# Attention with beacons and a gated MLP on one core: merged softmax sums, shared product banks, early score chunks in the ring, and a new order

## The chip, the cores and the metric

One core of a Trainium2 chip runs the whole program. The metric is the device time of one execution in microseconds; the time of the kernel before is the median of three runs.

## The reference

Eight batches of eight heads attend over 576 tokens of 64 channels, with 16 beacon keys and values in front that every query sees; the heads are laid side by side, and an MLP with a sigmoid-gated activation follows.

```python
B, H, S, Nb, D = (8, 8, 576, 16, 64)
k_all = np.concatenate([beacon_k, k], axis=2)
v_all = np.concatenate([beacon_v, v], axis=2)
scores = scale * np.matmul(q, k_all.transpose(0, 1, 3, 2))   # causal beyond the beacons
a = np.exp(scores); a /= a.sum(-1, keepdims=True) + 1e-09
attn = np.matmul(a, v_all)                                   # -> x: 4608 x 512
h = x @ w_in                                                 # 512 x 2048
g = h * (1.0 / (1.0 + np.exp(-1.702 * h)))
out = g @ w_out                                              # 2048 x 512
```

## The kernel before

**Work and tiles.** The kernel computes in f16 with sums in f32. Attention goes in 16 sets of four heads (two sets a batch). Per set, the loads bring keys, queries (`kn`, `qn`) and values (`vb`), cast on the way by POOL's DMA queue; DVE transposes them to `kT`, `qT`, and casts and transposes the beacon keys (`e_bk`, `e_turn`). The scores are computed transposed (keys on partitions, queries on columns), in chunks of 512 columns for four heads at once (L484): 32 rows of the array per head, four heads side by side. A chunk lies in one tile `s` of four PSUM banks; ACT takes the exp of it into `E` (L495), and the next chunk waits for that. Masks are cut in by POOL (L516), for the first sets partly by DVE (L509). The value products and the softmax sums (L571, operands `vb` or `ones`) use 32 columns of the array per head. DVE turns the sums out of PSUM (L583), takes reciprocals (L590), spreads them (L594), and normalises the products into `xT` (L606).

From the fifth set on (`s >= EARLY`) the key blocks of `E` are first added on DVE (`e_zadd`, L534), and a set's sums are two products, one for queries 0 to 223 and one for 224 to 575, each with its own transpose, reciprocal and spread.

**The MLP** runs in groups of tokens, two of 256 and then of 512. `w_in` products (L630) go through a gate: for the first two groups tanh on ACT (L644) and a product on DVE (L663), later a Gelu activation (L651), which needs another table in ACT than exp. The second product is plain for the first two groups (L675). For the others it is a 2x2 scheme with seven products in place of eight (`products`, L744): DVE builds sums of the quarters (`e_s`, L695), each of products 1 to 7 fills a PSUM bank of its own, and DVE adds the banks into output tiles (`e_half` on ACT, `e_join` at L760), from where SP stores them. The last three groups use such a scheme for `w_in` too (`fast`: L831, L841, L850, L853, L859).

**PSUM** has eight banks: a ring of four (`u0` to `u3`) for sums, value and MLP products, and four for `s`, which join the ring once the last chunk is done.

**Order.** Every operation is entered in a plan with its engine, a duration and its dependencies. `ORDER` lists each engine's operations in the order in which they are emitted; the list was made beforehand, and `Plan.run` only merges the five lists by planned times and gives out the banks. So the order on each engine is fixed in the code, and an engine that waits holds up all behind it. POOL's queue holds the loads too: each waits for the one eight places before it to land.

**Fill.** Matmuls on a constant tile (L1326) are put ahead of the first two chunks: 72 of 112 columns and 2 of 256 columns in f32.

Of the kernel before, what the change touches and what calls it, by code (L numbers as in the profile page):

```python
# [7 lines left out]
F16 = mybir.dt.float16  # L8
F32 = mybir.dt.float32
# [8 lines left out]
        76, 100, 115, 118, 120, 106, 138, 141, 143, 108, 155, 111, 152, 129, 161, 158, 122, 131, 164, 167, 134, 127,  # L18
        170, 173, 176, 145, 125, 148, 150, 177, 182, 188, 191, 227, 194, 197, 232, 183, 203, 234, 200, 178, 237, 179,
        206, 258, 241, 209, 184, 263, 185, 212, 265, 213, 248, 246, 268, 214, 215, 401, 251, 253, 272, 218, 404, 275,  # L20
        244, 279, 219, 220, 407, 282, 284, 277, 221, 414, 320, 296, 304, 290, 302, 292, 300, 298, 312, 308, 294, 318,
        314, 310, 306, 316, 426, 435, 423, 343, 338, 339, 340, 433, 431, 438, 344, 345, 359, 349, 341, 464, 346, 350,
        351, 352, 354, 574, 355, 429, 360, 361, 577, 356, 362, 357, 372, 365, 583, 474, 477, 373, 366, 374, 367, 605,
        480, 484, 375, 482, 607, 368, 506, 502, 488, 492, 610, 490, 486, 498, 504, 500, 508, 514, 510, 516, 494, 496,
        512, 534, 593, 596, 535, 536, 539, 540, 550, 541, 542, 537, 742, 545, 546, 547, 548, 603, 745, 551, 552, 553,
        599, 601, 619, 622, 748, 555, 556, 557, 558, 561, 755, 625, 627, 629, 562, 563, 776, 568, 564, 569, 570, 571,
        779, 764, 767, 659, 637, 641, 657, 649, 651, 647, 661, 635, 631, 653, 805, 772, 770, 774, 643, 655, 633, 639,
        645, 679, 680, 815, 818, 700, 681, 682, 684, 701, 915, 690, 685, 686, 691, 692, 702, 918, 687, 693, 695, 703,
        696, 924, 821, 823, 697, 698, 706, 946, 825, 707, 713, 708, 709, 948, 934, 937, 714, 715, 716, 827, 951, 944,
        940, 942, 853, 831, 833, 855, 857, 851, 843, 835, 837, 847, 839, 845, 829, 849, 841, 1083, 960, 963, 875,  # L30
        876, 880, 877, 878, 881, 882, 1086, 968, 966, 970, 883, 1089, 902, 909, 903, 886, 891, 1096, 887, 888, 889,
        892, 893, 1117, 904, 894, 905, 896, 897, 1120, 898, 899, 910, 911, 1105, 1108, 1146, 912, 976, 994, 996, 972,
        978, 1000, 1002, 992, 984, 990, 986, 988, 974, 980, 982, 998, 1168, 1111, 1115, 1159, 1113, 1156, 1025, 1026,
        1020, 1027, 1171, 1021, 1022, 1028, 1023, 1031, 1177, 1032, 1033, 1164, 1166, 1162, 1199, 1034, 1036, 1047,
        1048, 1037, 1201, 1041, 1042, 1038, 1039, 1233, 1049, 1204, 1043, 1044, 1050, 1235, 1237, 1054, 1055, 1056,
        1057, 1239, 1249, 1190, 1241, 1265, 1251, 1242, 1253, 1255, 1187, 1245, 1267, 1258, 1281, 1257, 1269, 1216,
        1195, 1197, 1193, 1213, 1261, 1271, 1285, 1287, 1283, 1273, 1289, 1274, 1219, 1221, 1223, 1334, 1290, 1293,
        1277, 1357, 1335, 1313, 1318, 1314, 1336, 1315, 1319, 1316, 1320, 1321, 1373, 1324, 1325, 1337, 1326, 1329,
        1327, 1361, 1377, 1375, 1330, 1359, 1340, 1331, 1341, 1332, 1363, 1342, 1366, 1365, 1379, 1381, 1347, 1382,
        1348, 1369, 1389, 1385, 1349, 1343, 1395, 1393, 1391, 1405, 1350, 1397, 1398, 1409, 1437, 1407, 1411, 1413,  # L40
        1401, 1414, 1481, 1438, 1417, 1497, 1442, 1443, 1444, 1483, 1439, 1440, 1499, 1487, 1501, 1485, 1458, 1445,
        1459, 1460, 1489, 1513, 1490, 1448, 1453, 1449, 1450, 1451, 1454, 1503, 1455, 1493, 1505, 1461, 1456, 1464,
        1465, 1517, 1515, 1506, 1529, 1519, 1509, 1466, 1471, 1522, 1472, 1473, 1521, 1533, 1467, 1474, 1582, 1525,
        1535, 1537, 1531, 1538, 1561, 1566, 1562, 1541, 1588, 1567, 1589, 1563, 1564, 1568, 1569, 1572, 1590, 1573,
        1574, 1575, 1591, 1577, 1578, 1595, 1579, 1580, 1583, 1584, 1585, 1596, 1597, 1598,
    ],
    "ACT": [
        1, 3, 77, 79, 103, 101, 107, 109, 112, 153, 156, 130, 159, 162, 132, 165, 168, 135, 171, 174, 189, 192, 228,
        195, 198, 233, 235, 201, 204, 238, 180, 207, 259, 210, 264, 186, 266, 269, 216, 402, 405, 408, 222, 417, 415,
        297, 291, 303, 305, 301, 299, 293, 309, 321, 295, 319, 313, 315, 311, 307, 317, 436, 439, 342, 465, 468, 575,  # L50
        578, 584, 587, 606, 608, 503, 507, 489, 491, 493, 487, 499, 505, 509, 515, 517, 495, 501, 511, 497, 513, 611,
        538, 743, 746, 749, 756, 758, 777, 780, 660, 642, 638, 652, 658, 648, 650, 636, 632, 662, 654, 806, 644, 634,
        656, 640, 646, 809, 916, 683, 919, 928, 925, 947, 949, 952, 828, 832, 854, 856, 852, 858, 834, 838, 844, 840,
        836, 846, 830, 848, 850, 842, 1084, 879, 1087, 1090, 1099, 1097, 1118, 1121, 1147, 1150, 977, 995, 997, 973,
        979, 1001, 993, 985, 991, 989, 1003, 975, 981, 987, 983, 999, 1169, 1172, 1024, 1181, 1178, 1200, 1202, 1234,
        1205, 1236, 1238, 1240, 1250, 1252, 1244, 1266, 1254, 1256, 1268, 1248, 1246, 1264, 1270, 1260, 1282, 1262,
        1272, 1286, 1284, 1288, 1276, 1280, 1292, 1294, 1296, 1278, 1358, 1317, 1374, 1378, 1376, 1360, 1362, 1364,
        1372, 1380, 1368, 1370, 1384, 1390, 1386, 1396, 1394, 1406, 1388, 1392, 1410, 1408, 1412, 1404, 1400, 1416,
        1402, 1482, 1418, 1420, 1498, 1484, 1500, 1441, 1486, 1488, 1496, 1492, 1502, 1504, 1494, 1514, 1516, 1508,
        1518, 1520, 1512, 1510, 1530, 1528, 1534, 1524, 1526, 1536, 1532, 1540, 1544, 1542, 1565,  # L60
    ],
    "DVE": [
        73, 74, 75, 97, 98, 99, 80, 81, 82, 78, 116, 105, 87, 104, 117, 102, 121, 119, 139, 140, 144, 142, 157, 154,
        123, 163, 160, 124, 224, 169, 128, 166, 172, 175, 146, 147, 126, 149, 151, 225, 226, 398, 190, 193, 196, 199,
        255, 256, 257, 202, 205, 286, 242, 411, 287, 211, 208, 243, 399, 249, 247, 400, 250, 412, 254, 252, 273, 245,
        274, 280, 276, 413, 281, 285, 283, 278, 289, 461, 288, 462, 419, 580, 420, 463, 326, 327, 328, 421, 322, 92,
        323, 324, 422, 427, 428, 424, 425, 325, 330, 334, 329, 335, 432, 336, 331, 434, 337, 332, 333, 470, 347, 582,
        353, 471, 581, 472, 430, 473, 358, 363, 475, 476, 478, 479, 481, 485, 739, 483, 369, 376, 370, 589, 752, 740,
        590, 615, 518, 753, 921, 519, 754, 526, 591, 527, 520, 528, 592, 529, 521, 741, 522, 597, 523, 594, 530, 595,
        598, 531, 802, 532, 524, 533, 616, 543, 525, 604, 549, 617, 618, 554, 600, 620, 602, 623, 624, 621, 559, 760,  # L70
        628, 761, 762, 626, 630, 565, 763, 566, 768, 572, 765, 811, 812, 766, 803, 804, 769, 773, 771, 671, 1080,
        775, 672, 813, 922, 663, 814, 664, 675, 667, 816, 673, 819, 668, 669, 817, 923, 665, 666, 820, 674, 676, 677,
        1093, 670, 688, 694, 678, 930, 822, 824, 699, 931, 826, 932, 933, 704, 710, 938, 939, 935, 936, 717, 711,
        945, 941, 943, 1081, 956, 957, 958, 871, 1082, 1094, 1095, 959, 872, 873, 1225, 867, 859, 961, 962, 964, 965,
        860, 863, 1174, 1143, 861, 874, 862, 868, 864, 967, 865, 971, 866, 969, 884, 869, 870, 1101, 1144, 890, 1145,
        1102, 895, 1226, 1103, 1104, 900, 906, 1109, 907, 1110, 913, 1106, 1107, 1152, 1153, 1227, 1176, 1175, 1154,
        1012, 1004, 1005, 1155, 1006, 1112, 1116, 1008, 1160, 1016, 1013, 1009, 1157, 1161, 1007, 1114, 1158, 1017,
        1010, 1011, 1014, 1029, 1018, 1183, 1165, 1163, 1019, 1229, 1015, 1230, 1035, 1228, 1231, 1167, 1184, 1040,
        1232, 1209, 1045, 1185, 1051, 1052, 1186, 1058, 1210, 1191, 1243, 1192, 1247, 1211, 1212, 1188, 1189, 1263,
# [28 lines left out]
    ],  # L108
}


class Op:
    __slots__ = (
        "eng", "dur", "deps", "pr", "due", "emit", "kind", "ring", "mode", "lat",
# [4 lines left out]
class Plan:  # L119
# [30 lines left out]
    def run(self):  # L150
# [25 lines left out]
        while any(todo.values()):  # L176
            first = None
            for e, seq in todo.items():
# [15 lines left out]
                if first is None or t < first[0]:  # L194
                    first = t, e, i
# [1162 lines left out]
```

## Time and profile before

| | |
|---|---|
| median of 3 runs | 324.87 us (324.68 to 325.06) |
| profiled execution | 324.84 us, of which the span of its instructions 323.1 us |
| mean granted TensorE clock | 0.992 |
| busy: PE, DVE, ACT, POOL | 312.2 (97%), 261.7 (81%), 219.5 (68%), 113.4 (35%) us |
| table loads of ACT | 14, of 1283 ns |
| first score chunk, first MLP matmul | 8.27 us, 17.21 us |

PE is TensorE's matmul, PEld its weight loads, DVE VectorE, ACT ScalarE, POOL GpSimd, SP SyncE. A line of the profile names the source line, the engine, the operation, output and inputs, the shape and the count, then busy time or start and duration, and in brackets the idle time before it and what ended that.

### The profile page before, as it was taken

The numbers are of one execution on the slowest core, as the hardware profiler recorded it, in microseconds if no ns is written. First come the engines' busy times: TensorE is split into PE (matmuls) and PEld (weight loads), VectorE is DVE, ScalarE is ACT, GpSimd is POOL, SyncE is SP. The second block draws the span as 40 slices with busy tenths as digits, with TensorE's granted clock in tenths as the row PEclk, the third lists the DMA queues.
The fourth block names the chain that finished last, engine by engine and source line by source line (L and its number), as shares of the span: only waits on it lengthen the run. The fifth ranks groups of instructions, "written<-read, shape, count | busy, mean of one in ns | idle before, by whom it ended". The sixth has DMA issues, their size and how long they took to land. (4 is left out here: it accounts for less than half of the span.)

```text
span 323.1 us, 10371 instructions
## 1 busy us (share of the span) xinstructions
PE 312.2 (97%) x4508; PEld 230.0 (71%) x4508; DVE 261.7 (81%) x524; ACT 219.5 (68%) x272; POOL 113.4 (35%) x178
## 2 busy tenths in 40 slices
PE   7689999999999999999999999999999999999994
PEld 7467665644776467745878877646888888888884
DVE  4837798777987989976998889986999895585784
ACT  1676597677767686689767696768778735974830
POOL 8775478190328403871058208600221000000000
PEclk9899999999999999999999999999999999999998
DMA  7999999294423941396019908900111001101112
GB/s 124 163 200 208 206 185 184 54 97 85 123 70 66 185 73 34 53 183 89 2 36 134 189 3 80 176 28 2 37 34 65 4 32 34 67 2 36 65 67 97
DMA packets 58222, 28.85 MB, mean 89 GB/s; under 512 B 41280, under 2 KB 53568, under 8 KB 58176
## 3 DMA queue, kind: packets, MB, share of 16 engines
q0 software_dynamic: 47552, 18.49, 48.4%
q1 hardware_dynamic: 10560, 9.69, 9.3%
q8 instruction: 35, 0.57, 0.7%
q14 instruction: 11, 0.09, 0.1%
q10 hardware_dynamic: 64, 0.01, 0.0%
HBM read 37.22 MB, written 9.44 MB: 144 GB/s over the span
## 5 line engine op out<-in xcount | busy, mean ns | idle before, releaser
L495 ACT ACTIVATE E<-s 128x2048 f16<-128x2048 f32 (+5 forms) x66 | 98.9, 1515 | 41.4 <-PE s L484 40.9
L630 PE MATMUL u<-xT,w 128*128 128x256 f16 (+1 forms) x512 | 87.3, 326 | 0.6 <-ACT g L651 0.5
L516 POOL TENSOR_SCALAR_AFFINE_SELECT E<-E 128x512 f16<-128x512 f16 (+3 forms) x78 | 48.8, 658 | 107.5 <-ACT E L495 94.2
L630 PEld LDWEIGHTS <-w 128*128 128x128 f16 x512 | 49.0, 98 | 34.7 <-issue 1.9
L651 ACT ACTIVATE g<-u 128x512 f16<-128x512 f32 x80 | 43.2, 599 | 15.6 <-PE u L630 15.4
L744 PEld LDWEIGHTS <-g 128*128 128x128 f16 x512 | 48.5, 98 | 7.1 <-issue 0.3
L744 PE MATMUL u<-w,g 128*128 128x256 f16 x384 | 49.9, 273 | 0.0
L760 DVE SCALAR_TENSOR_TENSOR osb<-u,osb 128x512 f32<-128x512 f32 x56 | 37.6, 683 | 13.6 <-PE u L744 11.7
L484 PEld LDWEIGHTS <-kT 32*128 32x128 f16 x1376 | 25.6, 93 | 20.6 <-issue 12.1
L744 PEld LDWEIGHTS <-sA 128*128 128x128 f16 x384 | 36.3, 98 | 5.1 <-issue 0.3
L484 PE MATMUL s<-qT,kT 32*128 32x32 f16 (+20 forms) x1376 | 34.9, 230 | 3.9 <-ACT E L495 2.0
L859 ACT ACTIVATE g<-u 128x512 f16<-128x512 f32 x48 | 26.9, 602 | 12.4 <-PE u L831 6.8
L744 PE MATMUL u<-tB,sA 128*128 128x256 f16 x256 | 34.9, 273 | 0.1
L606 DVE TENSOR_TENSOR xT<-u,rz 128x352 f16<-128x352 f32 (+2 forms) x52 | 25.8, 518 | 7.4 <-PE u L571 7.1
L415 POOL DMA_DIRECT2D vb<-in_v_dram x32 | 27.4, 876 | 2.2 <-DMA qn<-in_q_dram 1.2
L571 PE MATMUL u<-E,vb 128*32 128x352 f16 (+8 forms) x928 | 27.9, 265 | 0.0
L534 DVE TENSOR_TENSOR zs<-zs,E 128x1344 f16<-128x1344 f16 (+2 forms) x36 | 22.6, 628 | 2.3 <-POOL E L516 1.6
L571 PEld LDWEIGHTS <-vb 128*32 128x32 f16 (+1 forms) x928 | 19.8, 97 | 5.5 <-issue 1.5
L455 DVE STREAM_TRANSPOSE kT<-kn 128x576 f32<-128x576 f32 x16 | 20.1, 1258 | 2.3 <-DMA kn<-in_k_dram 1.5
L831 PE MATMUL u<-xT,w 128*128 128x256 f16 x144 | 20.5, 273 | 0.0
L831 PEld LDWEIGHTS <-w 128*128 128x128 f16 x192 | 18.8, 98 | 2.2
L455 DVE STREAM_TRANSPOSE qT<-qn 128x576 f32<-128x576 f32 x16 | 19.9, 1241 | 0.1
(73 smaller groups left out, 397.5 us busy)
## 6 DMA issues: line engine op xcount, KB each, us to landing
out_dram<-osb SPq DMA_DIRECT2D x36, 256.0 KB, 2.3
kn<-in_k_dram POOLq DMA_DIRECT2D x16, 288.0 KB, 6.3
qn<-in_q_dram POOLq DMA_DIRECT2D x16, 288.0 KB, 6.8
vb<-in_v_dram POOLq DMA_DIRECT2D x24, 128.0 KB, 6.6
w<-in_moe_w_in_dram POOLq DMA_DIRECT2D x8, 256.0 KB, 9.6
w<-in_moe_w_out_dram POOLq DMA_DIRECT2D x4, 512.0 KB, 13.8
vb<-in_v_dram POOLq DMA_DIRECT2D x8, 112.0 KB, 5.0
vb<-in_v_dram POOLq DMA_DIRECT2D x8, 80.0 KB, 7.8
```

The costliest lines, as they stand in the source:

```text
L415: nc.gpsimd.dma_start(out=t[0 : hi - lo, j, h0:h1, :], in_=v[b, h0:h1, lo:hi, :].rearrange("h n d -> n h d"),)
L455: nc.vector.transpose(out=f32(dst.rearrange("p n e -> p (n e)")).rearrange("p (r t) -> p t r", t=TR), in_=f32(src[:, :]).rearrange("p (t c ...
L484: nc.tensor.matmul(sc[:, h, o : o + w], kT[s % NB2][r : r + 32, j * P : (j + 1) * P, d], qT[s % NB2][r : r + 32, a : a + w, d], start=(d = ...
L495: nc.scalar.activation(out=Es[s][:, :, c0:c1], in_=ss[i][:, :, o : o + c1 - c0], func=AFT.Exp, scale=0.125,)
L516: nc.gpsimd.affine_select(out=blk, in_=blk, compare_op=ALU.is_ge, fill=0.0, base=off + (Nb if j == 0 else 0), pattern=[[0, Q], [1, w]], ch ...
L571: nc.tensor.matmul(u[32 * h : 32 * h + 32, a:e], lhs, src[0:kw, h, col : col + e - a], start=first, stop=last,)
L630: nc.tensor.matmul(u[:, o + a - t0 : o + e - t0], w1t[:, kp, nt * P : (nt + 1) * P], xT[:, kp, a % XR : (e - 1) % XR + 1], start=(kp == 0) ...
L651: nc.scalar.activation(out=gts[g][:, n0:n1, 0:w], in_=rings[("m1", g, n0)][:, 0 : n * w].rearrange("p (n w) -> p n w", n=n), func=AFT.Gelu ...
L744: nc.tensor.matmul(u[:, HM * mt : HM * (mt + 1)], lhs[:, n, mt * P : (mt + 1) * P], rhs[:, n, :], start=(n == 0 and mt == 0), stop=(n == H ...
L760: nc.vector.scalar_tensor_tensor(out=osbs[(g, dst)][:, :], in0=rings[("p", g, p)][:, :], scalar=scale_of(g), in1=osbs[(g, src)][:, :], op0 ...
L831: nc.tensor.matmul(u[:, HM * n : HM * (n + 1)], lhs[x][:, (2 * i + n) * P : (2 * i + n + 1) * P], rhs[:, x, :], start=fresh and n == 0 and ...
L859: nc.scalar.activation(out=gts[g][:, n : n + 2, HM * h : HM * (h + 1)], in_=rings[src][:, :].rearrange("p (n w) -> p n w", n=2), func=AFT. ...
```

## The change

- **Merged sums.** From the fifth set on, both halves of 288 queries go into one bank of 288 columns. `ones` becomes 64 columns wide with zeros in columns 32 to 47; as weights, columns 32 to 63 put the second half's sums on rows 16 to 31 of each head's block, and columns 16 to 47 the first half's on rows 0 to 15. One transpose, one reciprocal (18 values) and one spread (576 columns) serve the set, and all its value products wait for this one.
- **Shared product banks.** Product 3 is added by PE into the bank of product 5, after the join that makes the block c22 has read it; one join of a group's seven goes. Products 5 and 4 change places. The four output tiles of a group are set up together.
- **Ring chunks.** The second and third chunk (`RINGED`) put each head's scores into a ring bank, with one exp per head; later chunks wait for the last chunk in `s` alone. Only the first chunk's exp is still split in two.
- **Fill.** While the plan's PE time is under 20 us, gaps get matmuls of 256 columns: 34, 17, 3 and 3 of them come out.
- **Order.** The plan now counts a later landing for most q/k and v loads and keeps some DVE operations (beacon casts, sums) and POOL's masks apart; all five lists of `ORDER` are new. In POOL's queue the loads of the third set's queries, the second batch's beacon values and, later, three more q/k loads come ahead of weights. ACT's program has 16 table loads in place of 14.

```diff
+HELD = ("s", "zadd", "xsum", "wsum", "t", "mask", "bk")
...
+        if eng == "POOL" and name.startswith("mask"):
+            o.port = 2
+        elif eng == "DVE" and name.rstrip("0123456789") in HELD:
+            o.port = 1
...
+                if o.port:
+                    t = max(t, held[3 - o.port])
...
+        if d.eng == "Q" and d.name[:4] in ("ldqk", "ldv1", "ldv2", "ldv3", "ldv4", "ldv5", "ldv6", "ldv7"):
+            if d.name not in ("ldqk0q", "ldqk1q", "ldqk2q", "ldqk3q"):
+                return 5400
...
-    FILL = {"qk0": ((72, 112, F16),), "qk1": ((2, 256, F32),)}
+    FIRST, WARM, COLS = 3800, 20000, 256
...
+    RINGED = (1, 2)
...
-        sc = upper_pool(f"pss{plan.late_of(i)}").tile([P, Q, 512], F32, tag="s", name="s")
-        ss[i] = sc
+        if i in RINGED:
+            ss[i] = [ring_tile(("qk", i, h)) for h in range(Q)]
+        else:
+            sc = upper_pool(f"pss{plan.late_of(i)}").tile([P, Q, 512], F32, tag="s", name="s")
+            ss[i] = [sc[:, h, :] for h in range(Q)]
+            sall[i] = sc
...
-            if half:
-                return [[2, P, 0, S - HA, zsum[s], HA - Z0, True, True, 0]]
             return [
-                [2, P, Z0, HA, zsum[s], 0, True, True, 0],
-                [2, P, 32, Z0, E, 32, True, True, 0],
-                [2, P, 0, 32, E, 0, True, True, 0],
+                [3, P, 0, HF, zsum[s], HF - Z0, True, False, 0],
+                [2, P, Z0, HF, zsum[s], 0, False, True, 0],
+                [2, P, 32, Z0, E, 32, False, True, 0],
+                [2, P, 0, 32, E, 0, False, True, 0],
             ]
...
+                    lhs = ones[0:kw, 32:64] if x == 3 else ones[0:kw, 16:48]
...
-        u = ring_tile(("p", g, p))
+        u = ring_tile(("p", g, {3: 5}.get(p, p)))
...
-                    start=(n == 0 and mt == 0),
+                    start=(n == 0 and mt == 0 and p not in (3,)),
...
-        prod(4)
-        c21 = join(4, "u", "b", [u3])
-        store(c21, "b", 1, 0)
         prod(5)
-        u4 = join(5, "m", "m", [u3], False)
-        c22 = join(5, "u", "u", [c21, u4])
-        store(c22, "u", 1, 1)
-        prod(3)
-        c12 = join(3, "m", "m", [u4])
+        c22 = join(5, "u", "b", [u3], False)
+        store(c22, "b", 1, 1)
+        prod(4)
+        c21 = join(4, "u", "u", [c22])
+        store(c21, "u", 1, 0)
+        prod(3, 5, [c22])
+        c12 = join(3, "m", "m", [u3], at=5)
         store(c12, "m", 0, 1)
...
+        if o.eng == "PE" and o.start < WARM:
+            free = [(max([0] + [c.end for c in plan.closers.get(x, ())]), i) for i, x in enumerate(held)]
+            since, i = min(free)
+            n = int((2.0 if until > FIRST else 1.8) * (o.start - max(until, since + 200)) / COLS)
+            if n > 1:
+                idle = psu.tile([P, 512], F32, tag=f"u{i}", name=f"u{i}")
+                for _ in range(n):
+                    nc.tensor.matmul(idle[:, 0:COLS], scrap[:, 0:P], scrap[:, 0:COLS], start=True, stop=True)
```

## The prediction

> **What bounds the kernel now.** The page comes first: which engine is full, and where not.
>
> ```profile
> span 323.1 us, 10371 instructions
> PE   7689999999999999999999999999999999999994
> PEclk9899999999999999999999999999999999999998
> DMA  7999999294423941396019908900111001101112
> ```
>
> TensorE (PE) is full but for the first three slices and the last; the DMA engines are full from the second to the seventh slice, 8 to 56 us. A busy PE need not be PE at its peak, so the windows by stage come next.
>
> ```profile
> core 0: us, PE busy (x), PEclk, DMA share, GB/s
> 0.00:8.00 8.00, 6.14 (x72) 1.00 0.73 122
> 8.00:16.00 8.00, 5.26 (x145) 0.87 1.69 164
> 16.00:24.00 8.00, 6.83 (x144) 0.92 1.32 199
> 24.00:256.00 232.00, 230.93 (x3584) 1.00 0.64 94
> 256.00:316.00 60.00, 60.00 (x566) 1.00 0.12 41
> ```
>
> From 24 us on PE idles for 1.07 us in 232 and then not at all. What is left to win lies in the first 24 us, where all 72 matmuls of the first row are fill and the clock drops, or inside the busy time. The timeline shows the first.
>
> ```profile
> 11.36 0.64 PE L484 MATMUL s<-qT,kT 32*128 32x288 f16 x24 [1.39 <-DVE qT L455]
> 12.07 1.94 ACT L495 ACTIVATE E<-s 128x896 f16<-128x896 f32 x2 [1.15 <-PE s L484]
> 14.06 0.83 PE L484 MATMUL s<-qT,kT 32*128 32x288 f16 x24 [0.94 <-ACT E L495]
> 14.95 1.45 ACT L495 ACTIVATE E<-s 128x1536 f16<-128x1536 f32 x1 [0.94 <-PE s L484]
> 17.21 1.32 PE L630 MATMUL u<-xT,w 128*128 128x256 f16 x8
> ```
>
> PE waits for ACT's exp to empty the one score tile, then ACT waits for PE's next chunk: 0.94 us each way. The chain of waits shows what is lost inside the busy time.
>
> ```profile
> 206.65 0.59 PE s L484 x28
> 207.24 0.55 PE u L744 x4
> 207.79 13.97 PE u L630 x64
> ...
> 263.17 0.44 PE u L831 x4
> ```
>
> Four full-array matmuls take 0.44 us among their like and 0.55 next to a score chunk (L484, 32 rows of the array); the same chain shows 0.54 beside a value product (L571, 32 columns). Each change of kind costs 0.10 to 0.11 us of a PE that reads busy.
>
> **The change, part by part.**
>
> *Merged sums.* Twelve sets lose a transpose out of PSUM, a reciprocal and a spread. Rows by shape: L583 536 + 405 ns become one of 477 (128x288); L590 219 + 187 become about 275 (18 values, 8 ns more each); L594 545 + 411 become about 780 (576 wide, 1.05 ns a column). That is 12 x (464 + 131 + 176) = 9.3 us of DVE. PE streams the same 576 columns per set. DVE is 81% busy and PE idles 1.07 us past 24 us, so nothing of it is on the path.
>
> *Shared product banks.* Product 3 adds into product 5's bank, and 8 of the 56 joins at L760 go: 8 x 683 ns = 5.5 us of DVE, off the path as well. The price is that product 3 waits until the join of c22 has read the bank. While other products stand between, as in all groups but the last, that is hidden. In the last group product 4 (16 matmuls, 1.75 us) stands between, while product 7's end, two joins of 0.69 and the hand-overs (0.34 and about 0.2) take some 1.9: +0.1, between 0 and 0.3. The tail itself stays as these rows have it, one join after the last matmul:
>
> ```profile
> 316.48 3.34 DVE L760 SCALAR_TENSOR_TENSOR osb<-u,osb 128x512 f32<-128x512 f32 x5 [1.93 <-PE u L744]
> 317.59 1.47 PE L744 MATMUL u<-w,sA 128*128 128x256 f16 x12
> ```
>
> *Ring chunks, fill and casts: the first 24 us.* I walk the new order with the old rows. The second chunk's queries are still the last to be transposed, so it starts at 11.4 as now. Its scores go to the four ring banks, the next chunk's to the score tile at once, and ACT then runs without gaps: four exps of 512 (0.59 us, 0.49 apart, as two of L644 in 1.08) to 14.1, then piece by piece 15.5, 16.2, 17.6, 18.4, 19.7. The sums come later, after the fifth chunk, at 16.1; behind them DVE has two chains of transpose 0.48, reciprocal 0.2, spread 0.48, and four normalisations of 0.4, to 20.4. The first MLP matmul so starts at about 20.9, against 17.21. Yet at 23.2 PE has behind it all 8 early chunks, 6 first-half and 2 second-half value groups and 2 MLP tiles; before, at 23.5, it had 6 chunks, 6 groups and 4 tiles. Two chunks (0.54 each) and two groups (0.56: three in 1.68) less two tiles (0.87) are +0.45, and 0.28 earlier: 0.7 us gained, between a loss of 0.8 (the walk late by one exp) and a gain of 2.2. The fill hides in waits: 34 matmuls of 256 columns before the first chunk, at the old fill's 86 ns per 112 columns 6.7 us, end at about 8.6, when the first chunk is ready (8.5: the same four transposes of 1.1 to 1.26 in another order); 17 after it (0.109 each) end at 10.9. Sixteen beacon casts only change places; one took 1.33 us of DVE at 40.55 for a mean of 0.34, beside a mask on POOL, and no one waited: nothing on the path.
>
> *Fewer changes of kind.* Fill left aside, the built program has 152 changes between the three kinds of matmul before and 130 after. Past the point of the last paragraph 140 are left before and 121 after: 19 x 0.11 = 2.1 us on the path. Bounds: 0.09 and 0.125 by pair of kinds, 1.7 to 2.4.
>
> *Loads in another order.* Key and query loads move ahead of weights in POOL's one queue, which the DMA row shows full. The second weight load of the old order's last four (w2) was issued at 26.77 and landed after the longest time of L428, 15.8: 42.6. Ahead of it the new order has three more q/k loads (288 KB each) and 208 KB of values. At the old mean rate (7.16 MB by 42.6 from the first bytes at about 4.1: 186 GB/s) it lands at 48.5. PE, dense from 20.9, asks for it at about 47.7. The earlier pieces come out alike: fifth and sixth w1 load at 25.5, asked for at 24.9; w2's third at 44.3, asked for at 44.0. The first wait shifts all later needs, so I count it once: +0.6, from 0 to 6 (below).
>
> *Table loads.* ACT's program has 16 in place of 14. These rows show one:
>
> ```profile
> 65.68 1.94 ACT L495 ACTIVATE E<-s 128x1536 f16<-128x1536 f32 x2
> 67.63 1.28 ACT L651 ACT_TABLE_LOAD   x1
> 68.93 1.08 ACT L651 ACTIVATE g<-u 128x512 f16<-128x512 f32 x2
> ```
>
> It is 1.28 us in a gap of 1.31. The waits show PE held by ACT's gelu once, 0.49 us (at 69.58, behind this load); behind the other loads the four banks of the ring covered it. Two more: +0.15, from 0 to 1.0. [...]
>
> *Sum.* -0.7 - 2.1 + 0.1 + 0.6 + 0.15 = -1.95 us. The profiled execution took 324.84 us (span 323.1 and 1.74 around it), 0.03 below the median of 324.87. Forecast: 322.9 us. About 0.2%, 0.65 us, is what a measurement can tell from no change.
>
> **The rivals.**
>
> *The load queue becomes the bound (slower).* The order on PE is fixed, so it stands at the w2 pieces near 41, 44 and 48 us if they are late. For it: the DMA row has no slack from 8 to 56 us, more bytes now stand ahead of w2 (8.26 MB for 7.16), and the window of 8 to 16 us moved 164 GB/s. Against it: the next windows moved 199 to 209, and POOL's waits for weights were 2.3 us in one place. At 172 GB/s the last piece lands at 52.1, 3.8 late: 322.9 + 3.8 - 0.2 already counted = 326.5. It decides from a landing at 50.5, which is 178 GB/s.
>
> *The early overlap is worth more.* If the sums do not wait for the fifth chunk's exp as I walked, and loads keep pace, the head gives its 2.2 and the 0.6 is not paid: 320.8. For it: ACT's idle of 0.94 to 1.15 us at each early chunk adds up to some 5 us. Against it: q, k and w1 land no sooner.
>
> *The clock falls for longer.* At half clock the chunk of 14.06 took 0.83, for 0.54 to 0.64 else. Fill stands at four places only; if the clock drops at 17 us, three chunks, six groups and two tiles pay 0.3, 0.2 and 0.87 each, 3.8 us, half of it in waits for ACT: 324.8, no change. [...]
>
> *The order gains nothing.* If a change of kind hides behind waits that now become visible, only the head is left, and it pays for the loads: 324.8, no change.
>
> **How the numbers follow.** Forecast case 0.56 (321.7 to 324.1 by its bounds), larger gain 0.14, the two cases of no change 0.10 together, slower by the queue 0.20. Faster by over 0.2% is 0.70, within it 0.10, slower 0.20. The range leaves out the best third of the larger gain and the slow case past its middle: 320.3 to 326.2.
>
> **What would show it.** Right: the first MLP matmul near 21 us and PE busy from there; PE idle past 24 us still about 1 to 2 us; the window of 24 to 256 us with more matmuls than 3584; DVE near 247 us busy; a tail of the same length. Wrong: waits of PE for w2 or w1 loads of over 1 us between 24 and 50 us; a granted clock below 0.9 in 16 to 24 us; new waits of PE for DVE beside L597 (merged sums) or for c22's join.

## The result: 1.2% slower

The changed kernel takes 328.44 us (median of 6 runs, 327.37 to 330.06) against 324.85 us (6 runs, 324.56 to 325.06) beside it: ratio 1.0118, interval 1.0089 to 1.0147. The forecast was 322.9, with 320.3 to 326.2 as its range. The profiled execution took 328.62 us, its span is 326.9; before it was 323.1. Runs of the changed kernel also spread over 2.7 us, those of before over 0.5. The ratios here and below leave out runs over 1.5% above the fastest run of the same kernel.

The page after, its slices in the same rows as before:

```profile
PE   7769999989999999999999999989999999999995
PEclk9997999999999999999999999999999999999998
DMA  7999999999006990975063375950012001011212
```

TensorE's row has three new dents: the third slice lower, an 8 at 65 to 73 us and an 8 at 212 to 220 us. The windows by stage give their sum (width, PE busy and matmuls, granted clock, DMA share, GB/s):

```profile
16.00:24.00 8.00, 5.34 (x198) 1.00 1.43 184
24.00:256.00 232.00, 228.57 (x3443) 0.99 0.67 94
```

Past 24 us PE idles for 3.43 us where it had idled for 1.07, and from 16 to 24 us for 2.66 where it had been 1.17. The DMA engines, busy to 56 us before, are now busy to 82 us: their share is 1.03 from 56 to 64 us and 1.52 from 72 to 80 us, where it was 0.36 and 0.43. The timeline of TensorE shows the first two dents:

```profile
16.05 0.55 PE L506 MATMUL s<-qT,kT 32*128 32x208 f16 x32 [0.81 <-ACT E L517]
...
18.48 0.21 PE L597 MATMUL u<-E,vb 128*32 128x48 f16 x4 [0.56 <-DMA vb<-in_v_dram]
...
21.91 0.83 PE L655 MATMUL u<-xT,w 128*128 128x256 f16 x6 [0.48 <-DMA w<-in_moe_w_in_dram]
24.36 2.01 PE L655 MATMUL u<-xT,w 128*128 128x256 f16 x10 [1.62 <-issue]
...
68.41 0.22 PE L506 MATMUL s<-qT,kT 32*128 32x48 f16 x6 [1.07 <-issue]
```

The words to read are the last: two pauses end by "issue", that is, by nothing that the profile records; between the matmuls' starts they are 1.89 and 1.25 us long. The first stands inside a bank's eight matmuls, after six of them, and all 16 in the two lines read the same two loads of weights, so nothing new is asked for there. Behind it the granted clock is half from 24.71 to 28.12 us (0.50 in the window of 26 to 28 us), and ten matmuls take 2.01 us. The third dent has a name, and the timeline of all engines shows why:

```profile
210.15 1.03 DVE L720 TENSOR_TENSOR qn<-qn,w 128x1024 f16<-128x1024 f16 x1
211.11 3.08 DVE L720 TENSOR_TENSOR kn<-kn,w 128x1024 f16<-128x1024 f16 x1
211.34 3.18 POOL L538 TENSOR_SCALAR_AFFINE_SELECT E<-E 128x512 f16<-128x512 f16 x5
...
214.11 0.68 DVE L785 SCALAR_TENSOR_TENSOR osb<-u,osb 128x512 f32<-128x512 f32 x1
...
214.84 7.50 PE L655 MATMUL u<-xT,w 128*128 128x512 f16 x34 [1.58 <-DVE osb L785]
```

VectorE is held for 3.08 us in one sum of weights, nearly as long as five masks run on GpSimd. The last join of group 5 stands behind it, and TensorE waits for the bank that this join frees. Before, the same two sums ran beside masks too, and neither was long:

```profile
202.72 1.58 POOL L516 TENSOR_SCALAR_AFFINE_SELECT E<-E 128x320 f16<-128x320 f16 x2
203.13 0.68 DVE L695 TENSOR_TENSOR qn<-qn,w 128x1024 f16<-128x1024 f16 x1
...
203.74 1.11 DVE L695 TENSOR_TENSOR kn<-kn,w 128x1024 f16<-128x1024 f16 x1
```

What the unexplained pauses have in common comes from the list of DMA transfers:

```profile
q8 instruction: 35, 0.57, 0.7%
```

I read these 35 transfers of 16 KB as TensorE's program, one for 256 of its instructions; the list names no engine, and the reading is worked out from the trace's counts: it has 8997 instructions of TensorE (a matmul is two, its weight load and itself), and 35 times 256 is 8960. Numbered in order, the pauses stand at instructions 704 and 2240, six times 256 apart, so I count group ends at 192, 448, 704 and so on (why not at 256 is not shown). The transfer for the next group had begun 2.25 and 2.24 us before the pause ended. Before, the shortest time from such a transfer's start to the first use of its code was 2.91 us.

To compare the kernels along the way, I count the columns that TensorE has streamed, fill left out and those of score and value matmuls at a quarter. The first column is when before reached some amount of work; the others say how much later (+) a run did, good to about 0.1 us, one matmul. The last three are the first, third and sixth kernel below.

| before at | changed | wide fill | join first | both, and loads |
|---|---|---|---|---|
| 20.98 | +1.05 | +1.93 | +1.26 | +1.30 |
| 24.68 | +3.87 | +1.43 | +2.61 | +1.60 |
| 60.82 | +3.11 | +1.06 | +1.83 | +1.06 |
| 72.16 | +3.50 | +0.21 | +2.23 | +0.21 |
| 207.84 | +2.99 | -0.27 | +1.72 | -0.27 |
| 214.90 | +4.47 | +1.21 | +1.46 | -0.53 |
| 318.79 (last matmul) | +4.00 | +0.76 | +1.00 | -0.98 |

Between the dents the changed kernel gains on before, as forecast; the dents take back more than all of it.

### The profile page after: what moved, and what is told of

It reads as the page before. It is cut to its first block, busy times and chain, and to the rows that moved or that the text cites. A ratio compares the mean times of both kernels' runs of the same rounds, so it can differ in the third digit from the quotient of the medians.

```text
span 326.9 us, 10282 instructions
## 1 busy us (share of the span) xinstructions
PE 312.7 (96%) x4489; PEld 230.9 (71%) x4489; DVE 249.3 (76%) x481; ACT 222.3 (68%) x279; POOL 114.6 (35%) x178
## 4 chain that ended last, share of the span: by engine, by line
PE 67%; ACT 2%; DVE 1%; issue 1%
PE u L769 29%; PE u L655 15%; PE u L856 11%; PE u L597 6%; PE s L506 5%; ACT g L676 1%; DVE osb L785 1%; ACT L676 0%; ACT L517 0%; ACT E L517 0%; DVE qn L720 0%; DVE xT L631 0%; DVE zt L607 0%; DVE kn L720 0%; DVE kT L466 0%
## 5 line engine op out<-in xcount | busy, mean ns | idle before, releaser
L517 ACT ACTIVATE E<-s 128x2048 f16<-128x2048 f32 (+5 forms) x63 | 95.6, 1532 | 42.3 <-PE s L506 40.4
L655 PE MATMUL u<-xT,w 128*128 128x256 f16 (+1 forms) x512 | 89.0, 329 | 4.0 <-issue 1.6
L538 POOL TENSOR_SCALAR_AFFINE_SELECT E<-E 128x512 f16<-128x512 f16 (+3 forms) x78 | 50.1, 662 | 116.6 <-ACT E L517 116.5
L655 PEld LDWEIGHTS <-w 128*128 128x128 f16 x512 | 49.9, 99 | 37.3 <-issue 4.8
L769 PE MATMUL u<-w,g 128*128 128x256 f16 x384 | 50.6, 273 | 0.1
L785 DVE SCALAR_TENSOR_TENSOR osb<-u,osb 128x512 f32<-128x512 f32 x48 | 33.0, 687 | 21.8 <-PE u L769 19.8
L506 PE MATMUL s<-qT,kT 32*128 32x32 f16 (+20 forms) x1328 | 33.6, 229 | 2.1 <-issue 1.1
L597 PE MATMUL u<-E,vb 128*32 128x208 f16 (+8 forms) x928 | 27.7, 262 | 0.9 <-DMA vb<-in_v_dram 0.6
L556 DVE TENSOR_TENSOR zs<-zs,E 128x1344 f16<-128x1344 f16 (+2 forms) x36 | 21.5, 598 | 1.9 <-POOL E L538 0.8
L720 DVE TENSOR_TENSOR sA<-g 128x512 f16<-128x512 f16 x32 | 12.8, 414 | 11.6 <-ACT g L676 11.6
```

What stands on the lines that cost most here:

```text
L506: nc.tensor.matmul(ss[i][h][:, o : o + w], kT[s % NB2][r : r + 32, j * P : (j + 1) * P, d], qT[s % NB2][r : r + 32, a : a + w, d], start=( ...
L517: nc.scalar.activation(out=Es[s][:, :, c0:c1] if h is None else Es[s][:, h, c0:c1], in_=sall[i][:, :, o : o + c1 - c0] if h is None else s ...
L538: nc.gpsimd.affine_select(out=blk, in_=blk, compare_op=ALU.is_ge, fill=0.0, base=off + (Nb if j == 0 else 0), pattern=[[0, Q], [1, w]], ch ...
L597: nc.tensor.matmul(u[32 * h : 32 * h + 32, a:e], lhs, src[0:kw, h, col : col + e - a], start=first, stop=last, skip_group_check=s >= EARLY ...
L655: nc.tensor.matmul(u[:, o + a - t0 : o + e - t0], w1t[:, kp, nt * P : (nt + 1) * P], xT[:, kp, a % XR : (e - 1) % XR + 1], start=(kp == 0) ...
L769: nc.tensor.matmul(u[:, HM * mt : HM * (mt + 1)], lhs[:, n, mt * P : (mt + 1) * P], rhs[:, n, :], start=(n == 0 and mt == 0 and p not in ( ...
```

## The experiments

Theory A: TensorE stands because its code has not arrived. Theory C: the join comes late because VectorE is held by the masks. Theory E: the order of loads costs the head 1 us. The rivals say that the pauses belong to the matmuls before which they stand (a weight or a bank), or that the wait for the join is replaced by another. All kernels below are edits of the changed one. The median of before was 324.88 us beside the first four, 325.24 beside the next four.

**The same fill in fewer instructions.**

```diff
-                for _ in range(n):
-                    nc.tensor.matmul(idle[:, 0:COLS], scrap[:, 0:P], scrap[:, 0:COLS], start=True, stop=True)
+                wide = [512] * (n // 2) if until == FIRST else [COLS] * n
+                for m in wide:
+                    nc.tensor.matmul(idle[:, 0:m], scrap[:, 0:P], scrap[:, 0:m], start=True, stop=True)
```

> Edit: the first fill is 17 matmuls of 512 columns in place of 34 of 256. It streams as many columns, so the head should not move, but TensorE's program is 34 instructions shorter from there on. Theory A (code arrives late): in the trace of the changed kernel TensorE's program is fetched in 35 transfers, one for every 256 instructions, and the two pauses named issue (1.89 us before instruction 704 at 24.36 us, 1.25 us before instruction 2240 at 68.41 us) both stand at instruction 192 of a group of 256, 2.25 and 2.24 us after such a transfer began. Shifted by 34 instructions the group ends fall behind the dense attention stretches; with a transfer that begins 3.9 us after the last group end, as before 45 us, and 2.25 us from there to the first use, no group end is late by more than 0.2 us. Both pauses go: 1.8 and 1.1 us less, and if the half clock from 24.7 to 28.1 us goes with the first pause, up to 1 us more. 325.5 us, from 324.5 to 326.5, and less spread between runs. Rival B (the first tile's matmuls wait for a weight piece or a bank there): the same two matmuls pause as long, 328.4 us.

Measured: 325.33 us (324.69 to 326.81, 12 runs), ratio to before 1.0016, interval 1.0004 to 1.0027. The same tile and the same score chunk in its timeline:

```profile
22.79 1.92 PE L655 MATMUL u<-xT,w 128*128 128x256 f16 x16
24.64 0.54 PE L506 MATMUL s<-qT,kT 32*128 32x208 f16 x32
...
31.11 0.42 PE L597 MATMUL u<-E,vb 128*32 128x288 f16 x9 [0.36 <-issue]
```

All 16 matmuls of the tile now run in one piece, and the pause at 68 us is gone too. The group now ends in the score chunk, at 24.76 us, and its code came just in time, 2.34 us after the transfer began. One short pause is new, at the next group end, 2.47 us after that transfer began: I had expected none later than 0.2 us. Seventeen pairs of instructions less, for matmuls that compute nothing, are worth 3.1 us. The half clock did not go, it came earlier (18.38 to 21.79 us; the granted clock is 0.79 from 16 to 24 us): the score chunk at 18.68 us took 0.83 us, the one at 22.32 us 0.54, and TensorE's coming later to 24.76 us helped the code to be in time.

**The fill in more instructions.** Ten of the 34 become sixteen of 128 columns: `wide = [COLS] * (n - 10) + [128] * 16 if until == FIRST else [COLS] * n`.

> Edit: of the first fill's 34 matmuls of 256 columns ten become sixteen of 128, so TensorE's program is 12 instructions longer from there on and streams 2 fill columns in 34 less. Theory A (code arrives late): the group ends move 12 instructions ahead, into the score chunks. The first pause then stands inside or before the attention matmuls between 21 and 24 us and the second near 67 us, and both are longer, since the matmuls ahead of them use up the code faster: by the same reckoning 0.4 us at about 18, 2.5 us at about 22, 2.9 us at about 67, part of the first two in place of waits there. 330 us, from 328.5 to 332. In the trace each such pause again ends 2.25 us after the start of a code transfer. Rival B (the first tile's matmuls wait for a weight piece or a bank): the pauses stay before the same two matmuls, 328.4 us, from 327.4 to 330.

Measured: 328.5 us (7 runs, 327.91 to 333.23), ratio 1.0099, interval 1.0085 to 1.0114. The time alone lies where the theories' ranges meet; the profiled execution (333.23 us, the slowest of the seven) tells them apart by place:

```profile
24.62 3.59 PE L655 MATMUL u<-xT,w 128*128 128x256 f16 x16 [3.24 <-issue]
...
71.62 0.33 PE L506 MATMUL s<-qT,kT 32*128 32x80 f16 x12 [2.18 <-issue]
```

The first pause moved six matmuls ahead, to the start of the tile, and the second six ahead in its score chunk (12 matmuls stand behind it, 6 before the edit). Both are longer, and they end 2.47 and 2.30 us after a transfer of code began. The rival had them stay. The pause that I expected at 18 us can't be told from the wait for values there (both would end at 18.42).

**The join first.** Operation 902 is the last join of group 5, 1196 the sums of weights, first `qn`, then `kn`.

```diff
-        1083, 1084, 1085, 880, 885, 1086, 890, 1088, 896, 1196, 902, 1151,
+        1083, 1084, 1085, 880, 885, 1086, 890, 1088, 896, 902, 1196, 1151,
```

> Edit: on VectorE the last join of group 5 (L785, at 214.11 us) goes ahead of the beacon weighting of two tiles (L720, qn and kn, at 210.15 us) that stood before it. Theory C (VectorE is held by GpSimd's masks): the second of these two operations took 3.08 us beside five masks of GpSimd, where its twin took 1.03, and TensorE waited 1.6 us for the bank that the join frees. With the join first it runs when the product ends at about 211.6, and the wait of TensorE for it goes: 1.5 us less, 326.9 us, from 326 to 327.7; one L720 still takes about 3 us beside the masks and nobody waits for it. Rival D (another wait takes its place: the ring's next bank is held by a gelu of ACT, which starts at 213.17 behind a table load): 0.3 us at most is won, 328.1 us.

Measured: 326.11 us (324.81 to 328.57, 12 runs), ratio 1.0054, interval 1.0033 to 1.0075. Its timeline at the join:

```profile
210.06 3.67 POOL L538 TENSOR_SCALAR_AFFINE_SELECT E<-E 128x512 f16<-128x512 f16 x5
210.10 4.26 PE L655 MATMUL u<-xT,w 128*128 128x512 f16 x19
210.31 0.69 DVE L785 SCALAR_TENSOR_TENSOR osb<-u,osb 128x512 f32<-128x512 f32 x1 [1.35 <-PE u L769]
...
211.75 1.06 DVE L720 TENSOR_TENSOR kn<-kn,w 128x1024 f16<-128x1024 f16 x1
```

TensorE no longer waits there: in the table the changed kernel loses 1.48 us from 207.84 to 214.90, this one gains 0.26. That is 1.74 us of the 3.0 between the two profiles; the other 1.26 lie at the head, where in this execution the clock never fell, though both pauses for code stand (1.94 and 1.26 us between starts). What the medians differ by beyond the join, some 0.6 us of 2.3, is not explained; the runs of the two kernels spread over 2.7 and 3.8 us. What I had wrong is the sum of weights: once it starts among the masks and not just ahead of them it takes 1.06 us, and the masks 3.67 in place of 3.18. This repeats: the sum took 3.08 or 3.09 us in all six profiles that keep the old order and 1.06 in all four with the join first. That the masks hold it is read from their place beside it; no run took them away.

**Values and weights first in the load queue.** In the lists of GpSimd and of landings the third set's queries (51) and the second batch's beacon values (61) go behind the first pair of weight pieces (27, 25).

> Edit: in GpSimd's queue the third set's queries and one load of the second batch's beacon values go behind the first values and the first pair of weight pieces of the first layer. Theory E (the load order costs the head about 1 us): TensorE waited 0.56 us at 18.48 for values that landed at 18.43 and 0.48 at 21.91 for weights that landed at 21.86, and the queue moves 288 KB in about 1.4 us, so both land about 1.4 us earlier and the two waits go. The first tile of the first layer starts at about 20.9 as I had walked it. If the end follows, 327.4 us, from 326.5 to 328. Rival A (code arrives late): the code of the next group is not there before 24.36 in any case, so all that is won ahead of it is lost again in a longer pause: 328.4 us, with the pause before instruction 704 some 2.5 to 2.9 us long.

Measured: 328.98 us (6 runs, 327.32 to 331.67), ratio 1.0133, interval 1.0099 to 1.0167: no gain. Its timeline:

```profile
21.63 0.83 PE L655 MATMUL u<-xT,w 128*128 128x256 f16 x6
24.36 1.27 PE L655 MATMUL u<-xT,w 128*128 128x256 f16 x10 [1.90 <-issue]
```

Both waits for loads are gone, and TensorE then stands at the same instruction until the same microsecond. What was won ahead of a group end was lost in waiting for its code, as the rival said. At the second group end it is the same: the pause there is 3.21 us between starts, in place of 1.25, and ends 2.34 us after its transfer began.

**Both cures, without and with the load order.**

> Edit: both the first fill of 17 matmuls of 512 columns and the last join of group 5 ahead of the beacon weighting. Theories A (code arrives late) and C (VectorE held by masks) take time from different places, so both gains should add: with the wide fill the run took 325.35 us and stood still 1.6 us for that join. 323.8 us, from 323.2 to 324.6: faster than before for the first time. Rival D (a slip of VectorE moves on to the next tile as PE comes earlier): the join's wait comes back in another place, 325.0.

> Edit: as the last one, and the first values and weight pieces go ahead of the third set's queries in GpSimd's queue. Theory E: in the run with the load order alone the waits for values and weights (0.56 and 0.48 us) were gone and the first tile started at 21.63 in place of 21.91, and the pause for code ate the rest. With the group ends shifted, code is there at about 24.7 at the latest either way, so at most 0.3 us is left of that: 323.5 us, from 322.8 to 324.4. If code is never late, up to 1 us less than without the load order: 322.8. Rival: TensorE reaches the next group end earlier than its code, a pause near 24 us returns: 324.5.

Measured: 323.32 us (5 runs, 322.81 to 324.52), ratio 0.994, interval 0.9926 to 0.9953; with the load order 323.35 us (5 runs, 323.32 to 323.6), ratio 0.9946, interval 0.9934 to 0.9959. Each alone took off 3.1 and 2.3 us; together it is 5.1, and both versions beat before. The load order's own part can't be told from nothing. In the profile without it no pause for code is left, but the clock is half from 17.64 to 24.46 us, where the score chunk at 22.97 us takes 0.83 us for 0.54. The window of the one with it that stands against 228.57 (x3443) above:

```profile
24.00:256.00 232.00, 231.03 (x3563) 1.00 0.67 94
```

**All four fills wide.** `wide = [512] * (n // 2)` everywhere, with the join and the load order: 30 pairs of instructions fewer.

> Edit: join first, load order, and all three fills of 512 columns, which takes 28 to 29 pairs of instructions out in place of 17. Theory A: the group ends move on by another 22 instructions. The end at 31.11 us, where the wide fill alone left a pause of 0.4 to 0.6 us, moves into matmuls of 0.109 us and its pause goes; the end at 24.76 moves the same way by about 0.3 us. 322.9 us, from 322.2 to 324. Rival: the earlier group end, near 19.3 us, now lies later than its code needs, and the next group is used up faster, so a pause of 0.5 us comes near 25: 323.6.

Measured: 323.41 us (5 runs, 323.4 to 323.69), ratio 0.9948, interval 0.9936 to 0.9961. As theory A said, the pause at 31 us went (0.11 between starts there); as the rival said, one came near 25, of 1.3 us at 25.13. Against the last kernel, 13 pairs of instructions fewer only chose which group ended late.

**Does the transfer of code queue behind data?** With the wide fill, up to 35 us a transfer begins 3 to 4 us after the group end before it; past 205 us, where the DMA engines have little to do (share 0.13 from 256 to 320 us, 1.42 from 16 to 24), at most 0.7 after and up to 2.5 ahead of it. The edit is the wide fill, and 36 more loads of queries behind GpSimd's last mask. The first attempt put them into tiles that the last groups still used:

> Edit: the wide fill, and 36 more loads of 288 KB of queries behind GpSimd's last mask, into tiles that nothing reads any more; they only fill the DMA engines from about 245 to 297 us, where the wide-fill run left them idle. Theory A in its detail (the transfer of code queues behind data): in that run a transfer began 3.2 to 3.9 us after the last group end up to 35 us, with the DMA engines full, and 2.5 us before to 0.6 us after it past 205 us. With the loads the transfers at about 261, 275 and 289 us begin 2 to 4 us after the group end, in place of 2.3, 0.9 and 2.5 us before it. No pause follows, since a group lasts 14 us there. 325.3 us as with the wide fill alone, at most 0.5 more. Rival F (TensorE asks late in the head for a reason of its own, such as short instructions, and data does not matter): the transfers begin where they did, within 0.7 us.

Measured: 367.66 us, since the loads began only at 302 us and outlasted the work by 40; one transfer fell among them, 1.06 us after its group end where it had been 1.69 ahead. The second attempt took the value tiles:

> Edit: the wide fill, and 36 more loads of 288 KB of queries at the end of GpSimd's program, this time into the value tiles, which nothing uses past the last value product at about 250 us (in the last attempt the tiles were in use until 302 us, so the loads came too late to answer). They only fill the DMA engines, and may lengthen the run at its end if they outlast it; its total is not the question. Theory A in its detail: in the wide-fill run, with idle DMA engines, the code transfers begin 2.3 us before the group end at 261.0, 0.9 before that at 275.0, 2.5 before 289.0 and 2.4 before 303.0. With the loads those that fall among them begin 1 to 4 us after the group end. Rival F (data does not matter, the head's transfers are late for TensorE's own reason): they begin within 0.7 us of where they did, before the group end.

Measured: 326.02 us (one run; before 324.46 beside it). The windows of 260 to 280 us show that the loads were there (DMA share 1.11 and 1.04; with the wide fill alone 0.08 and 0.01) and that TensorE had the same work:

```profile
260.00:270.00 10.00, 10.00 (x94) 8.96 (x92) 7.56 (x19) 7.99 (x16) 2.86 (x6) 1.00 1.11 187
```

Start of a code transfer, counted from the group end before it (us):

| group end near | 261 | 275 | 289 | 303 | 317 |
|---|---|---|---|---|---|
| wide fill | -2.30 | -0.86 | -2.48 | -2.42 | -1.69 |
| with the loads | +0.28 | +1.21 | -1.14 | -1.26 | +0.90 |

All five are later, by 1.2 to 2.6 us, 2.0 in the mean: in this run the loads delayed the code, and the rival falls. The two kernels with both cures, whose groups end at the same matmuls and which have no such loads, stay within 0.5 us of the first row at all five. The size fits in part: two of five still begin before the group end. At the head the transfers begin some 5.5 us later, counted from group ends, than in the first row; these loads explain 2 of that. Traffic is denser there (DMA share up to 1.5, here up to 1.1), and the instructions are shorter; which of the two makes the rest stays open.

## Why the prediction was wrong

- **What failed first: the fill "hides in waits".** Its time does. Its instructions do not: the prediction costed a stream of TensorE instructions by duration alone and never by count, so that waiting for code stood at nothing in the sum; it took 1.89 and 1.25 us. The new order also puts score and value matmuls (23 ns each in a row of 24 that takes 0.54 us) close together, so a group of 256 instructions lasted 5.7 us from 18.62 to 24.36, pause included, where the transfer of code began 3.5 us after the group end and the pause ended 2.25 after that. None of my four signs for "wrong" was this one: no load made PE wait over 1 us past 24 us, and the clock in 16 to 24 us was 1.00. The rivals (load queue, clock, no gain) did not hold it either. In eight kernels 14 pauses of 0.5 to 3.4 us between starts stand at such group ends, each ending 2.2 to 2.6 us after the transfer began. By count that is little, with some 35 group ends a profile and at most two or three such pauses; by cost it is not, since taking two of them away was worth 3.1 us.
- **The head, forecast at -0.7.** At the first MLP tile it was +1.05, by the 0.56 and 0.48 us of waits for values and weights; the walk, which had the first tile at 20.9, held no wait for either. Then the pause, 1.89, and the half clock behind it: the run with the join first, which has the same pause and no half clock, is 1.26 better at the next row. Together +3.87 by 24.68. With the cures and the load order +1.60 remain; 0.78 of it is a pause for code, and the half clock that it had from 17.58 to 20.99, and that the walk had not assumed, would be 1.26 by the two runs just compared. Taking both off leaves -0.4 for the walk's -0.7. This is an estimate, and no run shows the head without a pause and without half clock; the walk had no term for either.
- **"Nothing of it is on the path" for VectorE.** An engine 76% busy and ahead of need in the mean still made TensorE wait 1.58 us, by one operation queued ahead of a join. The clue was in the prediction: a cast that took 1.33 us for a mean of 0.34 beside a mask, dismissed since no one waited. The sum of weights took 3.08 us beside five masks of GpSimd, while the same sums took 0.68 to 1.11 beside other masks; what decides was not tried.
- **Fewer changes of kind, forecast at -2.1: right in size.** From 24.68 us to the last matmul the kernel with both cures goes from +1.60 to -0.98, a gain of 2.58, which also holds what table loads and joins did. That the changes alone made it was not tried apart.
- **Loads (+0.6), table loads (+0.15), tail (+0.1): none was paid where it was put.** Loads cost the two waits of the head instead. Past 24 us no wait of TensorE for weights is left over 0.2 us, nor one for a gelu behind the 16 table loads. At the tail the last product starts without a wait, so c22's join had read its bank in time, and one join follows the last matmul as before:

```profile
321.16 1.91 PE L769 MATMUL u<-w,sA 128*128 128x256 f16 x16
...
323.10 0.69 DVE L785 SCALAR_TENSOR_TENSOR osb<-u,osb 128x512 f32<-128x512 f32 x1 [1.06 <-PE u L769]
```

- **VectorE's load.** Forecast 247 us, measured 249.3, and 247.2 with the join first, where the long sum takes 1.06: merged sums and shared banks save what their rows said, off the path.

With both causes mended the kernel takes 1.8 to 1.9 us less than before beside it (323.3 to 323.4 for 325.24), where the sum said 1.95: the sum was that of a kernel whose code and joins arrive in time. That the two numbers are so close is luck in part. In the profile with both cures and the load order the head cost 1.60 where 0.7 were to be gained, the stretch behind it gained 2.58 for 2.1, and the 0.85 of the three prices was not paid where it stood.

## What to carry to other kernels

Where an engine pauses for "issue", number its instructions: if the pauses stand whole multiples of 256 apart, as they did here at 704 and 2240, suspect that it waits for code, and try fewer or longer instructions ahead of the dense stretch, or move a group's end (3.1 us here); another order of loads won nothing here. Count instructions as well as microseconds when a change packs short ones together while the DMA engines are full: here 256 went by in 5.7 us at a DMA share of 1.43. And put the join that frees a bank ahead of work that nobody waits for, on an engine with time to spare too; here it was worth 1.74 us in the profile.

## What was not expected of the hardware

- With loads of data running, five transfers of code began later, by 1.2 to 2.6 us.
- Half clock at the head lasted 3.413 us in the profiles of before and of the changed kernel, and began a whole number of such lengths after the first record of full clock. In the changed kernel that record begins at 7.64 us and half clock 17.07 us (5 x 3.413) later, 24.71 to 28.12; before, at 7.08 us and 6.83 us (2 x 3.413) later, 13.91 to 17.32. Two profiles with pauses of their own had none at the head: the join first (granted 1.00 in the windows to 24 us) and the second late loads (0.999 over the span). At 24.68 us in the table the join first, which has the same pause, stands 1.26 us better than the changed kernel.
- The stretch ahead of half clock held few columns. Counted as in the table above, but with the fill, and in steps of 3.413 us from the first record of full clock, the step just ahead of half clock at the head held 2560 columns in both profiles, before and changed, and the one ahead of half clock at the end of the work (from 321.11 and 325.08 us) 2816 in both; every other step at full clock in these two held 3024 or more. The pause of 1.89 us in the changed kernel lies whole in its step of 2560 columns, 21.29 to 24.71 us. That this half clock follows from the pause for code is my reading of these counts; no run tried it apart, and the one at 18.38 us with the wide fill had no such pause before it.
